# Top-k attention before two expert layers: one TensorE job for a block's transposes, a later block's scores and a query, and exponentials written to SBUF

## The chip, the core and the metric

The kernel runs on one core of a Trainium2 chip. A core has TensorE for matrix products (PE in the profile; its weight loads are a row of their own, PEld), VectorE (DVE), ScalarE (ACT), GpSimd (POOL) and a queue that issues transfers (SP). Each engine works through its own list of instructions in a fixed order; semaphores hold an instruction back until what it needs is there. TensorE writes into PSUM, which has eight banks of 128 x 512 fp32 values; everything else lives in SBUF. The metric is the device time of one execution in microseconds.

## What is computed

Attention with a top-32 mask, then two mixture-of-experts layers, all in fp32:

```python
scores = scale * np.matmul(q, k.transpose(0, 1, 3, 2))      # 2 batches, 8 heads, 576 x 576, head size 64
kth = np.partition(scores, -32, axis=-1)[..., -32:-31]
scores = np.where(scores >= kth, scores, -1e9)
attn = np.exp(scores - np.max(scores, axis=-1, keepdims=True))
attn = attn / (np.sum(attn, axis=-1, keepdims=True) + 1e-9)
x = np.matmul(attn, v)                                       # -> 1152 rows of 512
...
for e in range(8):                                           # first mixture: every row through every expert
    out += P[:, e:e + 1] * (np.maximum(x @ w1[e], 0.0) @ w2[e])
...
# second mixture: each row goes to its best expert, in eight groups
```

P comes from gate logits by an exponential and eight alternating normalisations of rows and columns.

## The kernel before

**Blocks.** Attention is cut into 72 blocks, numbered n from 0. A block is 128 query rows against all 576 keys of one head; where a sequence has only 64 rows left, one block holds 64 rows of two heads. `block` makes the scores of a block, `search` (for n of 16 and more; `search_first` before) finds the 32nd largest score of each row and turns the scores into weights, `values` multiplies the weights with v once all blocks of a pair of heads are through. Blocks 16 to 71 are those that the change touches.

**One block, step by step.** (1) A query tile is transposed on TensorE (128 columns, L257), and ACT and DVE split it into two parts of fp32r, a high and a low one (L598, L606). (2) Scores: two halves of 288 keys, each in a PSUM bank of its own, with two products each, one for each part of the query (four where the block holds two heads; L618); ACT copies each half into the SBUF tile `sc` (L623). (3) The search on DVE: four times the 8 largest (MAX8; L715, L721), and between them three times these 8 taken out (MATCH_REPLACE8, L719). (4) ACT writes the exponentials of each half into a PSUM bank (L728), and DVE multiplies each half with the mask, `e = (sc >= 32nd) * exponential`, with the sum over the row as a by-product (a SCALAR_TENSOR_TENSOR and the read of its accumulator, L730). (5) DVE adds the two sums and takes the reciprocal (L736, L738), ACT scales `e` (L739). (6) TensorE turns `e`: four transposes into one bank, a fifth of 64 rows into another (L257). (7) ACT copies the high parts out of both banks (`eth`, L769), and DVE (L773), or in some blocks GpSimd (L777), writes the low parts (`etl`, and `eth` for the fifth).

**PSUM.** There are four banks named `tp` for attention and four named `yp` for the experts. Early on one `tp` bank is given to the experts (the job of type X at the end of the loop in `visits_first`), so that blocks 16 to 71 share three.

**What stands beside attention.** While attention runs, `visit` feeds the first mixture's experts to TensorE: layer 1 in chunks of four products (L980), layer 2 (L1090), in fp32r, with three products for each pair of high and low parts. Its weights are split by ACT (L918) and GpSimd (L924), its hidden layer by ACT (L932) and DVE (L934). What is not done beside attention is done after it; the amount is the same.

**What sets the order.** Nothing runs in the order of the code: `job` hands a piece of work with an engine, a rank, an estimated cost, the jobs it depends on and the buffers it takes to a planner (`Order`). The planner goes forward in its own estimated time: of the jobs of an engine that can start first, the one of lowest rank is taken and written out, and a job holds its buffers until all that use it have ended in the plan. Attention's jobs rank by block number, the experts' at 1000 and above. Where TensorE would be idle for more than a set time in the plan, `busy` writes idle products in (`ones_b`, L294) that keep it at work and whose result nobody reads. The plan becomes each engine's fixed order; on the chip an engine waits at its next instruction until that can run.

Of the kernel before, what the change touches and what calls it, by code (L numbers as in the profile page):

```python
# [7 lines left out]
F32 = mybir.dt.float32  # L8
# [10 lines left out]
EPS = 1e-9  # L19
# [4 lines left out]
PARTIAL = 2  # L24
FILL = 390.0
# [187 lines left out]
class Net:  # L213
# [208 lines left out]
    def attention(self):  # L422
# [5 lines left out]
        self.attended = []  # L428
        for g, (b, tiles) in enumerate(GROUPS):
            made = []  # L430
            for pair in range(4):
# [20 lines left out]
            self.spans.append((c0, c1, made))  # L452
            for t in range(c0 // 128, -(-c1 // 128)):
                self.xdone.setdefault(t, []).extend(made)
        self.gate_logits()

# [122 lines left out]
    def block(self, x):  # L579
# [16 lines left out]
        def src():  # L596
            return p.t[:, :128].rearrange("p (a c) -> p a c", a=2) if two else p.t[:, :128]
        jh = self.job("ACT", n - 2.9, t_act(128), lambda: nc.scalar.activation(parts(0), src(), AF.Copy),  # L598
                      deps=[j], use=[p, qs])
        if 2 <= n < ALONE:  # L600
            jm = self.job("PE", n - 2.9, 0.12, lambda: nc.tensor.matmul(
                p.t[:, :128], self.minus, parts(0), start=False, stop=True, skip_group_check=True), deps=[jh], use=[p, qs])
            jl = self.job("ACT", n - 2.9, t_act(128), lambda: nc.scalar.activation(parts(1), p.t[:, :128], AF.Copy),
                          deps=[jm], use=[p, qs])
        else:
            jl = self.job("DVE", n - 2.4, t_dve(128), lambda: nc.vector.tensor_sub(  # L606
                parts(1), src(), parts(0).bitcast(F32)), deps=[jh], use=[p])
# [3 lines left out]
        got = []  # L611
        for half in range(2):
            ps = self.psa.box()

            def scores(half=half, ps=ps):
                for m, (s, k) in enumerate(terms):
                    w = qs.t[:, s, k, :] if two else qs.t[:, s]
# [1133 lines left out]
```

## Time and profile before

| | |
|---|---|
| three runs | 1181.81, 1182.82 (median), 1186.1 us |
| the profiled execution | 1184.28 us, of which 1182.5 us from the first to the last instruction |
| busy over the span: PE, PEld, DVE, ACT, POOL | 98%, 85%, 77%, 62%, 35% |
| mean granted clock of TensorE | 0.996 of full speed |
| the first mask of block 16 begins (L730) | 97.7 us |
| the first and the last transpose of `e` in blocks 16 to 71 | 104.37 us, 542.14 us |

A busy share is an average over stages that have different limits. Here the stretch from 104 us to 542 us, in which blocks 16 to 71 run, is to be read apart from what follows, in which DVE and ACT have far less to do. A matrix product counts as busy until its modelled end, which lies behind the start of the next one; how fast TensorE works is read from the distance between starts.

### The profile page before, as it was taken

Reading aid. Unit: us, or ns where it says so; the run is one execution under the profiler, and the core shown is the slowest. Engines: PE = TensorE matmul, PEld = TensorE weight load, DVE = VectorE, ACT = ScalarE, POOL = GpSimd, SP = SyncE. Lnnn points to the kernel's source line nnn. Section 1 sums busy time; section 2 is a strip of 40 time slices with the busy share of each in tenths; the row PEclk is TensorE's granted clock in tenths of the full one; section 3 lists DMA queues with packets and bytes.
Section 4 is the critical chain, followed back from the end, with each engine's and each line's share of the span. In section 5 each row is a group of like instructions: output and inputs, shape, how many; then the busy total and the mean of one; then the engine's idle time right before and its main releaser. Section 6 shows DMA issues by size and latency. Waiting matters only on the chain.

```text
span 1182.5 us, 20945 instructions
## 1 busy us (share of the span) xinstructions
PE 1159.9 (98%) x6619; PEld 1004.2 (85%) x6619; DVE 911.7 (77%) x2194; ACT 734.2 (62%) x1729; POOL 417.9 (35%) x387
## 2 busy tenths in 40 slices
PE   8998999999999999999999999999999999999997
PEld 5866889888888888878888889999999999798886
DVE  7999999999999999995745667754455556468883
ACT  7666889989888977876343335543333445158882
POOL 5464788877656745446000001000000000015541
PEclk9999999999999999999999999999999999999999
DMA  5457775755444664444545546653344444179970
GB/s 142 113 154 199 203 193 171 203 167 157 141 130 119 183 196 131 152 126 131 169 149 185 172 144 194 194 147 115 116 127 131 143 143 147 49 229 362 353 262 23
DMA packets 243032, 194.04 MB, mean 164 GB/s; under 512 B 67487, under 2 KB 186271, under 8 KB 242912
## 3 DMA queue, kind: packets, MB, share of 16 engines
q1 hardware_dynamic: 240656, 187.74, 53.1%
q0 software_dynamic: 1648, 4.73, 1.0%
q8 instruction: 54, 0.88, 0.3%
q14 instruction: 66, 0.54, 0.1%
q10 hardware_dynamic: 608, 0.15, 0.1%
HBM read 172.34 MB, written 20.80 MB: 163 GB/s over the span
## 4 chain that ended last, share of the span: by engine, by line
PE 67%; DVE 17%; issue 5%; ACT 4%; DMA 3%; POOL 2%; SPq 1%; POOLq 0%; another core or an unknown queue 0%; DVEq 0%; ACTq 0%
PE yp L980 23%; PE yp L1090 21%; PE tp L1090 6%; PE tp L980 4%; DVE wk L719 3%; PE tp L257 3%; DVE m L721 3%; PE tp L618 2%; PE tp L809 2%; DVE e L730 1%; DVE wk L665 1%; DVE m L667 1%; DVE hl L934 1%; PE yp L1335 1%; DVE m L715 1%
## 5 line engine op out<-in xcount | busy, mean ns | idle before, releaser
L1702 POOL DMA_INDIRECT disp<-acc,idx x9 | 10.6, 1173 | 465.0 <-DVE run L1698 465.0
L924 POOL TENSOR_TENSOR w0l<-ra,w0h 128x512 fp32r<-128x512 f32 x96 | 124.5, 1297 | 70.7 <-ACT w0h L918 67.5
L924 POOL TENSOR_TENSOR w1l<-rb,w1h 128x512 fp32r<-128x512 f32 x96 | 124.4, 1295 | 61.8 <-ACT w1h L918 54.9
L980 PE MATMUL yp<-xl,w0h 128*128 128x256 f32 (+2 forms) x680 | 142.3, 331 | 0.0
L980 PE MATMUL yp<-xh,w0h 128*128 128x256 f32 (+2 forms) x680 | 141.7, 330 | 0.2 <-ACT w0h L918 0.2
L980 PE MATMUL yp<-xh,w0l 128*128 128x256 f32 (+2 forms) x680 | 141.6, 330 | 0.0
L918 ACT ACTIVATE w0h<-ra 128x512 fp32r<-128x512 f32 x211 | 131.7, 625 | 0.0
L918 ACT ACTIVATE w1h<-rb 128x512 fp32r<-128x512 f32 x148 | 93.0, 629 | 55.4 <-PE yp L1090 47.5
L721 DVE MAX8 m<-wk 128x8 f32<-128x576 f32 x168 | 125.2, 752 | 1.0
L980 PEld LDWEIGHTS yp<-xh,w0h 128*128 128x128 f32 x680 | 113.9, 189 | 11.8 <-ACT w0h L918 0.5
L932 ACT ACTIVATE hh<-yp 128x256 fp32r<-128x256 f32 (+3 forms) x142 | 64.0, 451 | 96.0 <-PE yp L980 78.7
L980 PEld LDWEIGHTS yp<-xh,w0l 128*128 128x128 f32 x680 | 110.7, 189 | 6.5 <-POOL w0l L924 0.4
L980 PEld LDWEIGHTS yp<-xl,w0h 128*128 128x128 f32 x680 | 110.9, 190 | 6.0
L1090 PE MATMUL yp<-w1h,hh 128*128 128x512 f32 x280 | 114.4, 409 | 0.0
L934 DVE SCALAR_TENSOR_TENSOR hl<-yp,hh 128x256 fp32r<-128x256 f32 (+3 forms) x142 | 71.4, 503 | 54.7 <-ACT hh L932 53.9
L1090 PE MATMUL yp<-v,f 128*128 128x512 f32 x480 | 112.4, 392 | 0.0
L1090 PE MATMUL yp<-w1l,hh 128*128 128x512 f32 x280 | 110.2, 393 | 0.0
L1090 PE MATMUL yp<-w1h,hl 128*128 128x512 f32 x280 | 109.8, 392 | 0.0
L1090 PEld LDWEIGHTS yp<-v,f 128*128 128x128 f32 x480 | 89.9, 189 | 18.0
L918 ACT ACTIVATE v<-rb 128x512 fp32r<-128x512 f32 x65 | 40.7, 629 | 77.9 <-PE yp L1090 52.3
L719 DVE MATCH_REPLACE8 wk<-m,wk 128x576 f32<-128x576 f32 x112 | 83.3, 744 | 0.5
L921 DVE TENSOR_TENSOR w0l<-ra,w0h 128x512 fp32r<-128x512 f32 x115 | 79.1, 688 | 1.0
(486 smaller groups left out, 2720.5 us busy)
## 6 DMA issues: line engine op xcount, KB each, us to landing
rb<-in_moe_w_dram SPq DMA_DIRECT2D x248, 256.0 KB
ra<-in_moe_w_dram SPq DMA_DIRECT2D x245, 256.0 KB
acc<-in_moe_w_dram SPq DMA_DIRECT2D x67, 256.0 KB
y<-ys SPq DMA_DIRECT2D x31, 256.0 KB
ys<-y SPq DMA_DIRECT2D x21, 256.0 KB
vr<-in_v_dram SPq DMA_DIRECT2D x40, 128.0 KB
disp<-z SPq DMA_DIRECT2D x6, 771.0 KB
qg<-in_q_dram SPq DMA_DIRECT2D x63, 64.0 KB
```

Source lines behind the costliest of these rows:

```text
L257: self.nc.tensor.transpose(out, in_, self.ident[:p, :p])
L618: nc.tensor.matmul(ps.t[:, :288], w, keys[k][0].t[:, half * 288:(half + 1) * 288], start=m == 0, stop=m == len(terms) - 1)
L719: j = self.job("DVE", r, 0.73, lambda i=i: nc.vector.match_replace(wk.t, m.t[:, i], flat() if i == 0 else wk.t, LOW), deps=[j], take=[wk] ...
L721: j = self.job("DVE", r, 0.66, lambda i=i: nc.vector.max(m.t[:, i + 1], wk.t), deps=[j], use=[wk] if i == 2 else [])
L809: nc.tensor.matmul(p.t[:, :nq], vs.t[:, t].rearrange("p a d -> p (a d)"), hd["et"].t[s][:, t, :nq], start=t == 0 and s == 0, stop=t == 4)
L918: jh = self.job("ACT", -500 + rank, t_act(512, True), lambda r=r, w=w: nc.scalar.activation(w.t[0], r.t, AF.Copy), deps=[j], take=[w])
L921: jl = self.job("DVE", -100 + rank, t_dve(512, True), lambda r=r, w=w: nc.vector.tensor_sub(w.t[1], r.t, w.t[0].bitcast(F32)), deps=[jh], ...
L924: jl = self.job("POOL", -100 + rank if k > 8 * NATIVE + 4 else FIRST - 3, t_pool(512), lambda r=r, w=w: nc.gpsimd.tensor_sub(w.t[1], r.t, ...
L932: jh = self.job("ACT", -1000 + k * 0.001, t_act(b - a), lambda: nc.scalar.activation(h.t[0][:, a:b], p.t[:, :b - a], AF.Relu), deps=deps, ...
L934: jl = self.job("DVE", -1000 + k * 0.001, t_dve(b - a), lambda: nc.vector.scalar_tensor_tensor(h.t[1][:, a:b], p.t[:, :b - a], 0.0, h.t[0] ...
L980: nc.tensor.matmul(p.t[:, :b - a], w1[0].t[i][:, d, :], self.xt[s][:, d, c0 + a:c0 + b], start=m == 0 and d == 0, stop=m == 2 and d == 3)
L1090: nc.tensor.matmul(y[t].t, h.t[i][:, c:c + 128], w2[0].t[s], start=f == 0 and m == 0, stop=f == last and m == 2)
```

## The change

From block 16 on, `search` no longer cuts the exponentials in halves: one ACT instruction writes all 576 into `e` in SBUF, and one DVE instruction masks `e` in place, with both its inputs, `sc` and `e`, in SBUF. The sum needs no addition of halves. The two PSUM banks that held the exponentials are not taken any more.

The new method `together(m)` makes one TensorE job of three things: the scores of block m+3 (both halves), the transpose of the query of block m+4, and the five transposes of `e` of block m, in this order. The query's transpose goes into columns 288 to 415 of the bank with the second half of the scores, the fifth transpose of `e` into the same columns of the bank with the first half. So a joint job takes all three `tp` banks at once, where seven single uses of a bank stood before. It can begin only when all its inputs and banks are there in the plan; what follows it (copies of scores, splits of query and of `e`) depends on the job as a whole. The jobs of `values` are now handed in behind the joint job of the last block of their heads.

```diff
--- before.py
+++ after.py
@@ -22,6 +22,8 @@
 GROUPS = ((0, (0,)), (0, (1,)), (0, (2, 3, 4)), (1, (0, 1)), (1, (2, 3, 4)))
 NATIVE = 2
 PARTIAL = 2
+AHEAD = 3
+GROUPED = AHEAD + 1
...
-                    made += self.values(b, pair, tiles, heads, n - 1)
+                    late.append((n - 1, lambda b=b, pair=pair, tiles=tiles, heads=heads, n=n, made=made:
+                                 made.extend(self.values(b, pair, tiles, heads, n - 1))))
...
+        for m in range(n - GROUPED, n):
+            self.together(m)
...
+    def together(self, m, query=None):
+        turn, rows = self.turns.get(m), self.rows_.pop(m + AHEAD, None)
+        if turn:
+            deps, take, use, cost, tail, _, jobs = turn
+            calls = []
+            tail.append(rows[2][0] if rows else self.psa.box())
+            take = take + ([] if rows else tail)
+            use = use + tail
+            if rows:
+                x, sc, ps, sdeps, stake, suse, scores, _ = rows
+                deps, take, use, cost = deps + sdeps, take + stake, use + suse, cost + 0.14 * 4 * len(x["heads"])
+                calls.append(scores)
+            go = jobs[0]
+            if query:
+                qdeps, qtake, quse, *_ = query
+                deps, take, use, cost = deps + qdeps, take + qtake, use + quse, cost + 0.13
+            def all_(calls=calls, go=go, query=query):
+                for f in calls:
+                    f()
+                if query:
+                    query[3]()
+                go()
+            j = self.job("PE", m, cost, all_, deps=deps, take=take, use=use)
+            if query:
+                query[4](j)
+            jobs[1](j)
+            if rows:
+                rows[7](j)
+        while self.late and self.late[0][0] <= m:
+            self.late.pop(0)[1]()
...
         qs = (self.qz if two else self.qs).box()
-        p = self.psa.box()
+        mine = n >= ROWS + GROUPED
+        p, at = (None, 288) if mine else (self.psa.box(), 0)
+        bank = [p]
         i = 0 if two else x["heads"][0]["i"]
-        j = self.job("PE", n - 3.5, 0.13, lambda: self.tr(p.t[:, :128], qg.t[:, i].rearrange("p s d -> p (s d)")),
-                     deps=[jq], take=[p, qs], use=[qg])
+        mid = []
+        def turn_q():
+            self.tr(bank[0].t[:, at:at + 128], qg.t[:, i].rearrange("p s d -> p (s d)"))
...
+        query = None
+        if not mine:
+            split_q(self.job("PE", n - 3.5, 0.13, turn_q, deps=[jq], take=[p, qs], use=[qg]))
+        else:
+            bank[0] = self.rows_[n - 1][2][1]
+            query = [jq], [qs], [qg, qs], turn_q, split_q
+        if mine:
+            self.together(n - GROUPED, query)
+        self.rows_[n] = (x, sc, banks, mid + [d for _, dd in keys for d in dd], [*banks, sc],
+                         [qs, sc] + [kb for kb, _ in keys], lambda: [scores(0), scores(1)], finish)
+        return
...
-        masks = []
-        for half in range(2):
-            p = self.psa.box()
-            je = self.job("ACT", r - 0.4, t_act(288, True, 1), lambda half=half, p=p: nc.scalar.activation(
-                p.t[:, :288], sc.t[:, half], AF.Exp, bias=st.t[:, 0:1], scale=0.125), deps=[jb, near], take=[p] if half else [p, e], use=[e])
-            masks.append(self.job("DVE", r, t_dve(288) + 0.08, lambda half=half, p=p: nc.vector.scalar_tensor_tensor(
-                e.t[:, half * 288:(half + 1) * 288], sc.t[:, half], m.t[:, 3, 7:8], p.t[:, :288], op0=OP.is_ge,
-                op1=OP.mult, accum_out=st.t[:, 1 + half:2 + half]), deps=[j, je],
-                use=[p, sc, e, m]))
+        je = self.job("ACT", r - 0.4, t_act(576, True, 1), lambda: nc.scalar.activation(
+            e.t, flat(), AF.Exp, bias=st.t[:, 0:1], scale=0.125), deps=[jb, near], take=[e], use=[e])
+        masks = [self.job("DVE", r, t_dve(576, True), lambda: nc.vector.scalar_tensor_tensor(
+            e.t, flat(), m.t[:, 3, 7:8], e.t, op0=OP.is_ge, op1=OP.mult, accum_out=st.t[:, 1:2]), deps=[j, je],
+            use=[sc, e, m])]
         def total():
-            nc.vector.tensor_scalar(st.t[:, 3:4], st.t[:, 1:2], st.t[:, 2:3], EPS, op0=OP.add, op1=OP.add)
+            nc.vector.tensor_scalar(st.t[:, 3:4], st.t[:, 1:2], EPS, None, op0=OP.add)
...
-        for t0, t1, rows in ((0, 4, 128), (4, 5, 64)):
-            p, nt = self.psa.box(), t1 - t0
-
-            def turn(p=p, t0=t0, t1=t1, rows=rows):
-                for t in range(t0, t1):
-                    self.tr(p.t[:rows, (t - t0) * 128:(t - t0 + 1) * 128], e.t[:, t * 128:t * 128 + rows])
...
+        p = self.psa.box()
+        fresh = [hd["et"] for hd in heads if "et_done" not in hd]
+        for hd in heads:
+            hd.setdefault("et_done", [])
+        tail = []
+        def turn():
+            for t in range(5):
+                rows, o, b = (128, t * 128, p) if t < 4 else (64, 288, tail[0])
+                self.tr(b.t[:rows, o:o + 128], e.t[:, t * 128:t * 128 + rows])
+        def split(j):
+            for t0, t1, rows in ((0, 4, 128), (4, 5, 64)):
+                nt = t1 - t0
+                b, o = (p, 0) if t0 == 0 else (tail[0], 288)
...
+        self.turns[n] = [[jn], [p] + fresh, [e], 0.11 * 5, tail, (None, None), (turn, split)]```

Counted over the whole program (one of the three ways in which the second mixture can go runs in an execution), the change removes 56 DVE and 56 ACT instructions; TensorE's real work is the same, with 47 idle products in place of 40.

The first place is TensorE's list around one block (tile `e_171`): the numbers behind the names are buffers, `qg` is a query tile, `kst` are keys, `qs` a split query, `w0`, `w1` and `h` belong to the experts. Before:

```order
L618 MATMUL tp_65<-kst_156,qs_163 128x288 x2
L257 MATMUL tp_66<-ident,e_171 128x128 x4
L1090 MATMUL yp_69<-w1h_87,hh_95 128x512
...
L257 MATMUL tp_65<-ident,e_171 64x128
L980 MATMUL yp_71<-xh,w0h_79 128x256 x4
...
L1090 MATMUL tp_67<-w1l_90,hh_97 128x512
L1090 MATMUL tp_67<-w1h_89,hl_98 128x512
L618 MATMUL tp_68<-kst_156,qs_163 128x288 x2
L257 MATMUL tp_65<-ident,qg_142 128x128
```

And now, at the same block:

```order
L1162 MATMUL yp_69<-w1h_89,hl_98 128x512
L1162 MATMUL yp_69<-w1h_87,hh_97 128x512
...
L1052 MATMUL yp_72<-xl,w0h_81 128x256 x4
L1052 MATMUL yp_72<-xh,w0l_82 128x256 x4
L667 MATMUL tp_65<-kst_156,qs_163 128x288 x2
L667 MATMUL tp_68<-kst_156,qs_163 128x288 x2
L259 MATMUL tp_68<-ident,qg_141 128x128
L259 MATMUL tp_66<-ident,e_171 128x128 x4
L259 MATMUL tp_65<-ident,e_171 64x128
L1162 MATMUL yp_69<-w1h_89,hh_93 128x512
```

The halves of the scores, the query and the two groups of transposes stood in five places with the experts' products between them, and now stand in one.

The second place is DVE's list around the masks of one block (`e_171`; `st` are the sums, `wk` and `m` the search, `hl` the experts' hidden layer). Before:

```order
L730 SCALAR_TENSOR_TENSOR e_171,st_181<-sc_168,m_177,tp_66 128x288
L719 MATCH_REPLACE wk_169<-m_174,sc_165 128x576
L730 SCALAR_TENSOR_TENSOR e_171,st_181<-sc_168,m_177,tp_65 128x288
L934 SCALAR_TENSOR_TENSOR hl_94<-yp_70,hh_93 128x256
L736 TENSOR_SCALAR st_181<-st_181 128x1
L721 MAX m_174<-wk_169 128x8
L738 RECIPROCAL st_181<-st_181 128x1
```

And now:

```order
L797 SCALAR_TENSOR_TENSOR e_171,st_181<-sc_168,m_177,e_171 128x576
L789 MATCH_REPLACE wk_169<-m_174,sc_165 128x576
L802 TENSOR_SCALAR st_181<-st_181 128x1
L844 TENSOR_TENSOR etl_185<-tp_66,eth_184 128x4x128
L844 TENSOR_TENSOR eth_184<-tp_65,eth_184 64x128
L804 RECIPROCAL st_181<-st_181 128x1
L1006 SCALAR_TENSOR_TENSOR hl_98<-tp_67,hh_97 128x256
```

One mask stands where two stood; the third operand was a bank, `tp`, and is `e` in SBUF.

The third place is where TensorE's list leaves the last block's transposes. Before:

```order
L1090 MATMUL tp_67<-w1h_91,hl_94 128x512
L257 MATMUL tp_65<-ident,e_171 128x128 x4
L257 MATMUL tp_68<-ident,e_171 64x128
L257 MATMUL tp_66<-ident,lgt 128x128
L980 MATMUL yp_70<-xh,w0h_83 128x256 x4
```

And now:

```order
L1052 MATMUL yp_71<-xl,w0h_83 128x256 x4
L1052 MATMUL yp_71<-xh,w0l_84 128x256 x4
L259 MATMUL tp_65<-ident,e_171 128x128 x4
L259 MATMUL tp_68<-ident,e_171 64x128
L1162 MATMUL yp_72<-w1h_91,hh_95 128x512
L1162 MATMUL yp_72<-w1l_92,hh_95 128x512
```

Counted from the start of the list to this point there were 684 layer-1 products of 256 columns and 672 layer-2 products; now there are 732 and 690 ahead of it, while those of other shapes, the scores (312), the products with v (198) and the transposes of `e` (360) are as many as before.

## Rows read from the trace of the kernel before

**Rows 1.** Busy time of each engine by stretch of the span.

```profile
core 0: us, PE busy (x) PEld busy (x) DVE busy (x) ACT busy (x) POOL busy (x), PEclk, DMA share, GB/s
...
104.37:542.14 437.77, 430.89 (x2571) 372.61 (x2572) 427.21 (x1148) 363.51 (x925) 288.19 (x271) 1.00 0.56 161
542.14:1182.50 640.36, 631.59 (x3448) 560.65 (x3446) 389.42 (x825) 300.01 (x592) 75.32 (x60) 1.00 0.53 169
```

**Rows 2.** DVE's waits, 97.7 to 542.14 us: total, times, longest; six lines.

```profile
DVE hl L934 <- ACT hh L932: 1.9, 1, 1.9
...
DVE prob L900 <- PE tp L257: 0.4, 1, 0.4
```

**Rows 3.** What weight loads waited for, 104.37 to 542.14 us.

```profile
PEld tp L257 <- DVE eth L773: 2.9, 5, 1.4
PEld tp L257 <- ACT e L739: 2.4, 4, 0.9
PEld tp L618 <- DVE etl L773: 1.9, 7, 0.4
...
PEld tp L618 <- DVE e L730: 1.4, 5, 0.5
```

**Rows 4.** Groups of TensorE instructions, 104.37 to 542.14 us.

```profile
L1090 PE MATMUL yp<-w1h,hh 128*128 128x512 f32 x168 | 70.0, 417 | 0.0
...
L980 PE MATMUL yp<-xl,w0h 128*128 128x256 f32 x196 | 32.7, 290 | 0.0
```

**Rows 5.** TensorE in order of time: start, length, instruction.

```profile
120.33 0.39 PE L1090 MATMUL tp<-w1h,hl 128*128 128x512 f32 x1
120.55 0.64 PE L980 MATMUL yp<-xh,w0h 128*128 128x256 f32 x4
121.03 0.64 PE L980 MATMUL yp<-xl,w0h 128*128 128x256 f32 x4
...
311.05 0.42 PE L618 MATMUL tp<-kst,qs 128*128 128x288 f32 x2
311.31 0.40 PE L1090 MATMUL yp<-w1h,hh 128*128 128x512 f32 x1
```

**Rows 6.** DVE in order of time around one block's masks.

```profile
315.23 0.50 DVE L730 SCALAR_TENSOR_TENSOR e<-sc,m,tp 128x288 f32<-128x288 f32 x1
...
315.65 0.51 DVE L730 SCALAR_TENSOR_TENSOR e<-sc,m,tp 128x288 f32<-128x288 f32 x1
...
316.09 0.29 DVE L606 TENSOR_TENSOR qs<-tp,qs 128x128 fp32r<-128x128 f32 x1
316.29 0.21 DVE L736 TENSOR_SCALAR st<-st 128x1 f32<-128x1 f32 x1
316.41 0.08 DVE L719 MATCH_VALUE_LOAD wk<-m,sc 128x8 f32 x1
```

**Rows 7.** DVE around a mask of 576 in SBUF (block 7).

```profile
51.27 0.80 DVE L685 SCALAR_TENSOR_TENSOR e<-sc,m,e 128x576 f32<-128x576 f32 x1
51.98 0.75 DVE L667 MAX8 m<-wk 128x8 f32<-128x576 f32 x1
```

**Rows 8.** DVE in the second mixture, both inputs in SBUF.

```profile
1060.99 1.36 DVE L1406 TENSOR_TENSOR xh<-acc,xh 128x512 fp32r<-128x512 f32 x1 [0.28 <-ACT xh L1400]
...
1064.00 0.67 DVE L1406 TENSOR_TENSOR xh<-acc,xh 128x512 fp32r<-128x512 f32 x1
...
1064.93 1.61 DVE L1406 TENSOR_TENSOR xh<-acc,xh 128x512 fp32r<-128x512 f32 x1
```

**Rows 9.** GpSimd in the same stretch.

```profile
1060.51 1.28 POOL L1403 TENSOR_TENSOR f<-acc,f 128x512 fp32r<-128x512 f32 x1 [2.31 <-ACT f L1400]
1064.70 1.30 POOL L1403 TENSOR_TENSOR xh<-acc,xh 128x512 fp32r<-128x512 f32 x1 [2.90 <-DVE xh L1406]
```

**Rows 10.** Groups of GpSimd instructions, 97.7 to 542.14 us.

```profile
L924 POOL TENSOR_TENSOR w0l<-ra,w0h 128x512 fp32r<-128x512 f32 x92 | 119.4, 1297 | 67.6 <-ACT w0h L918 64.4 <-DMA vr<-in_v_dram 1.0 <-POOL eth L777 0.8
L924 POOL TENSOR_TENSOR w1l<-rb,w1h 128x512 fp32r<-128x512 f32 x91 | 117.9, 1296 | 57.3 <-ACT w1h L918 50.3 <-PE tp L257 3.6 <-POOL eth L777 0.9
```

More of the change, by code (lines that the diff above doesn't have):

```diff
@@ L452, in attention @@
             self.spans.append((c0, c1, made))
+        for m in range(n - GROUPED, n):
+            self.together(m)
+        for c0, c1, made in self.spans:
             for t in range(c0 // 128, -(-c1 // 128)):
@@ L610, in block @@
         sc = self.sc.box()
-        got = []
-        for half in range(2):
[L613 to L617, printed above, removed]
-                    nc.tensor.matmul(ps.t[:, :288], w, keys[k][0].t[:, half * 288:(half + 1) * 288],
-                                     start=m == 0, stop=m == len(terms) - 1)
-            j = self.job("PE", n - 2 + 0.1 * half, 0.14 * len(terms), scores,
-                         deps=[jh, jl] + [d for _, dd in keys for d in dd], take=[ps] if half else [ps, sc],
-                         use=[qs, sc] + [kb for kb, _ in keys])
-            got.append(self.job("ACT", n - 1.9 + 0.1 * half, t_act(288), lambda half=half, ps=ps: nc.scalar.activation(
-                sc.t[:, half], ps.t[:, :288], AF.Copy), deps=[j], use=[ps, sc]))
@@ L625, in block, with scores, copied @@
-        (self.search_first if n < ROWS else self.search)(x, sc, got)
+        banks = [self.psa.box() for _ in range(2)]
+        def scores(half):
+            ps = banks[half]
+            for m, (s, k) in enumerate(terms):
+                w = qs.t[:, s, k, :] if two else qs.t[:, s]
+                nc.tensor.matmul(ps.t[:, :288], w, keys[k][0].t[:, half * 288:(half + 1) * 288],
+                                 start=m == 0, stop=m == len(terms) - 1)
+        def copied(half, j):
+            return self.job("ACT", n - 1.9 + 0.1 * half, t_act(288), lambda: nc.scalar.activation(
+                sc.t[:, half], banks[half].t[:, :288], AF.Copy), deps=[j], use=[banks[half], sc])
@@ new lines, in finish @@
+        def finish(j):
+            (self.search_first if n < ROWS else self.search)(x, sc, [copied(half, j) for half in range(2)])
+        if n < ROWS + AHEAD:
+            split_q(self.job("PE", n - 3.5, 0.13, turn_q, deps=[jq], take=[p, qs], use=[qg]))
+            got = []
+            for half in range(2):
+                j = self.job("PE", n - 2 + 0.1 * half, 0.14 * len(terms), lambda half=half: scores(half),
+                             deps=mid + [d for _, dd in keys for d in dd], take=[banks[1]] if half else [banks[0], sc],
+                             use=[qs, sc] + [kb for kb, _ in keys])
+                got.append(copied(half, j))
+            return (self.search_first if n < ROWS else self.search)(x, sc, got)
@@ new lines, in block @@
+        query = None
+        if not mine:
+            split_q(self.job("PE", n - 3.5, 0.13, turn_q, deps=[jq], take=[p, qs], use=[qg]))
+        else:
+            bank[0] = self.rows_[n - 1][2][1]
[4 more added lines that the diff above has]
+                         [qs, sc] + [kb for kb, _ in keys], lambda: [scores(0), scores(1)], finish)
@@ L781, in values @@
+        self.turns[n] = [[jn], [p] + fresh, [e], 0.11 * 5, tail, (None, None), (turn, split)]
     def values(self, b, pair, tiles, heads, n):
```

82 lines of the change are left out of this document (41 added, 41 removed).

## Prediction

> **What bounds the kernel now.** I read the stretches first [rows 1]. Between 104 and 542 us, while blocks 16 to 71 run, DVE is busy for 427.2 of 437.8 us, and TensorE's products look as full with 430.9. After 542 us TensorE is busy for 631.6 of 640.4 us and DVE for 389.4, so the rest of the kernel is TensorE's alone. Which of the two leads in the attention stage is seen from their waits. DVE hardly waits for anyone: six lines, from 1.9 us down to 0.4 us, 5.7 us together [rows 2]. TensorE's weight loads do wait, and mostly for DVE: for a bank that the split of the turned weights gives back (2.9 us for the transposes, 1.9 us for the scores), for a bank that a mask gives back (1.4 us), for the scaled `e` (2.4 us) [rows 3]. A second reading says the same. Where nothing is in the way, a layer-2 product takes 0.23 us up to the next start, four layer-1 products of 256 columns take 0.48 us, so one 0.12 us, and two scores 0.26 us, so one 0.13 us [rows 5]. The groups of [rows 4] are parts of 672 layer-2 products and 684 of those layer-1 products in this stretch; with each form counted at its own distance, TensorE's list from the first to the last transpose of `e` is worth 416 us. The 22 us between that and 437.8 are waits and restarts after them, hidden under the modelled ends. So in the attention stage DVE leads, TensorE follows with some slack, and a saving on DVE or a burden on it decides; outside the stage only TensorE's amount of work counts.
>
> One more fact of the order matters. The expert work is constant, so what is done beside attention is missing afterwards. The new list holds 48 more layer-1 products and 18 more layer-2 products before the last transposes of `e`: 48 x 0.12 + 18 x 0.23 = 9.9 us. The time of the whole therefore changes by what the stage's end changes, less 9.9 us.
>
> **The change part by part.**
>
> *Two masks become one.* Now two masks of 288 begin at 315.23 and 315.65 us and the next instruction begins at 316.09 us: 0.86 us a block [rows 6]. The trace has the new form twice in the first blocks, a mask of 576 with both inputs in SBUF: from 51.27 to the next start at 51.98 us, 0.71 us [rows 7]. That saves 0.15 us, in 56 blocks 8.4 us of DVE. Both have GpSimd idle beside them.
>
> *The sum of the halves goes.* The instruction stays, with one operand less. It takes 0.12 us up to the next start now [rows 6]; the saving lies between nothing and 6.7 us in all, and I take nothing, since what remains is an instruction on one column too.
>
> *The mask's second input moves from PSUM to SBUF.* This is the part that can cost. In the second mixture DVE subtracts 512 columns with both inputs in SBUF. One such takes 0.67 us at 1064.00 us. Two that begin while GpSimd is inside an instruction of its own take 1.36 and 1.61 us [rows 8]; GpSimd's two began at 1060.51 and 1064.70 us and ended at 1061.79 and 1066.00 us [rows 9]. Each time DVE ends 0.55 us after GpSimd does. So DVE stood still until GpSimd was through: 0.69 us more where 0.80 us of GpSimd's instruction was left, 0.94 us where 1.07 us was left, in short the remainder less 0.12 us. Before the change no mask of blocks 16 to 71 could meet this, since one input was a bank. In the stage GpSimd splits expert weights, 92 and 91 times 1.30 us [rows 10], which is 237 of 444 us. A mask that begins at any moment meets one with a chance of 0.53 and then waits 0.65 - 0.12 = 0.53 us: 0.28 us. GpSimd's other instructions, some 51 of the 288.2 us that it is busy [rows 1], are mostly shorter and add about 0.04 us. An estimate of 0.32 us a mask, 18 us for 56. The bounds are nothing, if the mask with its accumulator doesn't stand still as the subtractions do, and 30 us, if each mask meets a weight split. I take 18.
>
> The Trainium skill speaks of this in "SBUF — State Buffer", section "Who interferes with whom": a VectorE instruction with two inputs in SBUF takes its second one through a read interface that GpSimd shares, whoever starts first keeps it to its end, and an instruction with at most one SBUF input is not concerned. By that rule every mask pays and the old ones never did, which by the same row counts is the 18 us above; without it the mask would be the plain saving of 8.4 us. The traced subtractions agree with the rule; no row shows a mask beside GpSimd.
>
> *One exponential of 576 for two of 288.* ACT is busy for 363.5 us of the stage [rows 1] and no one's leader; what it saves is worth nothing here, being under DVE's work. If ACT led, it would be worth about what the joined mask saves on DVE, 8 us.
>
> *Five TensorE jobs become one.* The instructions are the same and none is cheaper: a product after a transpose costs its own length. What can go is waiting: seven uses of a bank become three, and the waits for masks' banks vanish. On the other side the job takes all three banks at once and stands behind the latest of its inputs, the scaled `e` of its block; the scores in it are wanted by DVE only three blocks later, so that DVE doesn't starve. As DVE leads, TensorE's lost waits buy nothing by themselves, except that DVE's own 5.7 us of waits for ACT's copies shrink. I take 2 us of them (bounds 0 and 5.7).
>
> *Seven more idle products*, 7 x 0.23 = 1.6 us, stand where the plan saw TensorE idle; in a stage that DVE leads they are covered by that idleness and cost nothing. Uncovered they cost 1.6 us.
>
> **The sum.** DVE's stage: - 8.4 + 18 - 2 = + 7.6 us. Less the 9.9 us of expert work that has moved into it: - 2.3 us. The profiled execution took 1184.28 us, 1.78 us more than its span and 1.46 us above the median of 1182.82. So 1182.0 us for that execution, 1180.5 us beside the median: I say 1181 us. A difference under 0.5%, 5.9 us, I count as no change; that is about what can be told apart here.
>
> **The rivals.**
>
> *TensorE leads (faster).* If masks don't stand still, or seldom, DVE has 427 - 8.4 = 419 us to do and TensorE 416 + 9.9 = 426 us. Then the joint jobs count: with one place to wait at in each block instead of five, and no bank given back by a mask, perhaps half of the 22 us of waits is left. Stage 426 + 11 = 437 us, 1 us less than now; with the 9.9 us and 1.6 us for idle products that is - 9 us, 1174 us beside the median. If a third of the waits is left, 1170 us; if none, 1162 us. For it speaks that waits for banks are the larger part of [rows 3]; against it, rows 8 and 9, where each subtraction that met GpSimd stood still.
>
> *The joint job passes DVE's halts on (slower).* The planner counts the mask at its undisturbed length and has already spent DVE's saving on the 9.9 us of expert work. A mask held up by 0.32 us delays the scaled `e`, the joint job behind which all of TensorE stands, layer 1 behind that, and DVE itself where it comes to the next split of a hidden layer; then nothing of the halts is made up in DVE's planned gaps, neither the 8.4 us nor the 2 us. The stage grows by the full 18 us: + 18 - 9.9 + 1.6 = + 9.7 us, 1193 us beside the median. It decides from the point on at which the halts are more than the 9.9 us plus the 5.9 us of the bound, some 0.28 us a mask, with nothing made up. Against it: the scores are three blocks ahead, and DVE's list has other blocks' searches between a mask and what waits for it.
>
> *The grouping does nothing*, since TensorE starts the same instructions and DVE sets the pace: this is inside my forecast, where its worth is 2 us.
>
> **How the numbers follow.** My forecast, halts on DVE and most of them paid for by the saving and the moved expert work, has 0.43 and covers 1175 to 1188 us, with halts from 12 to 24 us. TensorE leading has 0.33, 1165 to 1176 us; halts passed on, 0.24, 1188 to 1196 us. A range that leaves out no more than the outer parts of both, 2 in 10, is 1169 to 1193 us. Faster by over 0.5% means below 1176.9 us: 0.34, the first rival and the low end of the forecast. Slower, above 1188.7 us: 0.23. Between them 0.43.
>
> **What the profile after would show.** The mask's mean length should be about 0.8 + 0.3 us, spread from 0.8 to 2.1 us, the long ones ending a fixed time after a GpSimd instruction does; if all are 0.8 us, the first rival stands. DVE should be busy, halts included, for nearly all of the stage, and the last transpose of `e` should end near 550 us. Waits of weight loads for masks should be gone, and waits for the scaled `e` should have grown in their place. I should be wrong if TensorE's list turned out to wait for something that I hold to be early, such as keys, a query's transfer or the experts' weights from a GpSimd that DVE holds up in turn.

## The result, and the profile after

The changed kernel takes 1192.93 us (median of 6 runs, 1190.96 to 1193.24), the kernel before 1184.6 us on the same chip. The ratio is 1.0074, with a 95% interval of 1.0061 to 1.0088: slower by 0.74%, 8.8 us. I had said 1181 us and no change; the time lies at the very edge of my range, 1169 to 1193 us. The profiled execution of the changed kernel spans 1191.0 us, 8.5 us more than before. The first fence answers to [rows 1]: the stage, cut at the same 104.37 us, and what follows it.

```profile
104.37:561.67 457.30, 439.41 (x2642) 386.69 (x2639) 439.13 (x1042) 353.99 (x882) 309.68 (x277) 1.00 0.55 159
561.67:1191.00 629.33, 621.49 (x3381) 551.41 (x3379) 387.14 (x821) 293.30 (x580) 67.89 (x54) 1.00 0.53 168
```

The last transpose of `e` ends at 561.67 us instead of 542.14 us: 19.5 us later, where I had + 7.6. The rest of the kernel is 11.0 us shorter (640.36 to 629.33), as 9.9 us of moved expert work asked for. So what went wrong lies in the stage alone. DVE's column (the third behind the length) splits it: busy for 439.13 us (+ 11.9 on [rows 1]), idle for 18.2 us (+ 7.6).

DVE's waits between 104.37 and 561.67 us (total, times, longest) answer to [rows 2]; I had hoped to lose 2 us there:

```profile
DVE etl L844 <- ACT eth L840: 5.5, 4, 1.8
DVE m L785 <- ACT sc L671: 2.9, 6, 0.5
```

The first line is a low part that waits for ACT's copy of the turned weights, the second a search that waits for its scores: what the joint job delivers comes later than DVE could take it. The waits of the weight loads in the same stretch answer to [rows 3]:

```profile
PEld tp L667 <- DVE kst L569: 4.3, 5, 1.4
...
PEld tp L259 <- ACT e L805: 3.0, 5, 1.1
PEld tp L667 <- DVE eth L844: 2.8, 4, 1.2
PEld tp L667 <- DVE xr L886: 2.7, 4, 1.1
```

No wait for a mask's bank is left, as forecast. The wait for the scaled `e` has hardly grown (2.4 to 3.0 us). New are waits of the scores (L667), which now head the joint job, for DVE's splits of keys (`kst`) and for `xr`, a sum of `values`. Neither is an input that these scores were short of. The lists show what they wait for: ahead of such a wait DVE's last two key splits write `kst_151` and read banks `tp_68` and `tp_66`, and the joint job behind them writes its scores into `tp_68` and `tp_66`, from other keys (`kst_152`). All five waits for `kst` are of this kind, and the sum `xr` reads a bank too. The joint job waits for the last of its three banks. One place in order of time, from three engines:

```profile
145.76 0.23 DVE L569 TENSOR_TENSOR kst<-tp,kst 64x64 fp32r<-64x64 f32 x1
...
146.04 0.53 PE L667 MATMUL tp<-kst,qs 128*128 128x288 f32 x2 [1.15 <-DVE kst L569]
...
147.61 0.58 ACT L840 ACTIVATE eth<-tp 128x512 fp32r<-128x512 f32 x1
...
148.21 0.69 DVE L844 TENSOR_TENSOR etl<-tp,eth 128x512 fp32r<-128x512 f32 x1 [1.85 <-ACT eth L840]
```

The key split stands behind a mask that was halted (1.38 us from 144.33 us on), the joint job waits for its bank, and DVE then stands idle for 1.85 us until ACT has copied what the job turned.

The masks were halted as forecast. DVE and GpSimd in order of time (start, length) show one, as [rows 8, 9] did for other instructions:

```profile
206.95 1.69 DVE L797 SCALAR_TENSOR_TENSOR e<-sc,m,e 128x576 f32<-128x576 f32 x1
...
206.73 1.30 POOL L996 TENSOR_TENSOR w1l<-rb,w1h 128x512 fp32r<-128x512 f32 x1
207.98 1.82 POOL L996 TENSOR_TENSOR w0l<-ra,w0h 128x512 fp32r<-128x512 f32 x1
```

The mask begins 0.22 us after GpSimd's instruction and ends at 208.64 us, 0.61 us after that one's end at 208.03 us. GpSimd's next takes 1.82 us instead of 1.30: it stands still in its turn. The group of all 56 masks (sum, mean in ns):

```profile
L797 DVE SCALAR_TENSOR_TENSOR e<-sc,m,e 128x576 f32<-128x576 f32 x56 | 61.3, 1095 | 0.8
```

Undisturbed they take 46.1 us (run e9 below), so the halts are 15.2 us, 0.27 us each, where I had 18 us and 0.32. Of the 56 masks 25 take more than 1 us, and every one of these ends 0.61 or 0.62 us after an instruction of GpSimd does.

### The profile page after: what moved, and what is told of

The parts are those of the page before. It is cut to its first block, busy times and chain, and to the rows that moved or that the text cites. A ratio compares the mean times of both kernels' runs of the same rounds, so it can differ in the third digit from the quotient of the medians.

```text
span 1191.0 us, 20741 instructions
## 1 busy us (share of the span) xinstructions
PE 1157.4 (97%) x6626; PEld 1008.7 (85%) x6626; DVE 921.2 (77%) x2082; ACT 717.7 (60%) x1673; POOL 432.3 (36%) x387
## 4 chain that ended last, share of the span: by engine, by line
PE 55%; DVE 28%; ACT 5%; issue 5%; POOL 3%; DMA 3%; SPq 1%; POOLq 0%; DVEq 0%; ACTq 0%
PE yp L1162 18%; PE yp L1052 17%; DVE wk L789 6%; DVE m L791 5%; PE tp L1052 5%; PE tp L1162 4%; DVE e L797 3%; DVE hl L1006 2%; PE tp L259 2%; DVE m L785 2%; DVE wk L735 2%; DVE m L737 1%; DVE etl L844 1%; DMA ra<-in_moe_w_dram 1%; PE yp L1381 1%
## 5 line engine op out<-in xcount | busy, mean ns | idle before, releaser
L996 POOL TENSOR_TENSOR w0l<-ra,w0h 128x512 fp32r<-128x512 f32 x96 | 129.4, 1348 | 84.7 <-ACT w0h L990 79.1
L996 POOL TENSOR_TENSOR w1l<-rb,w1h 128x512 fp32r<-128x512 f32 x96 | 128.2, 1335 | 42.7 <-ACT w1h L990 33.2
L1052 PE MATMUL yp<-xh,w0h 128*128 128x256 f32 (+2 forms) x648 | 132.4, 326 | 1.3 <-DVE hl L1006 0.9
L1052 PE MATMUL yp<-xh,w0l 128*128 128x256 f32 (+2 forms) x648 | 131.7, 325 | 0.7 <-POOL w0l L996 0.7
L1052 PE MATMUL yp<-xl,w0h 128*128 128x256 f32 (+2 forms) x648 | 132.1, 325 | 0.0
L1052 PEld LDWEIGHTS yp<-xh,w0h 128*128 128x128 f32 x648 | 108.3, 188 | 13.5 <-DVE hl L1006 1.7
L1162 PE MATMUL yp<-w1h,hh 128*128 128x512 f32 x288 | 115.6, 401 | 1.2 <-ACT hh L1004 1.2
L1162 PE MATMUL yp<-w1l,hh 128*128 128x512 f32 x288 | 113.0, 392 | 0.4 <-POOL w1l L996 0.4
L1162 PE MATMUL yp<-w1h,hl 128*128 128x512 f32 x288 | 112.7, 391 | 0.0
L1162 PE MATMUL yp<-v,f 128*128 128x512 f32 x480 | 112.6, 392 | 0.0
L1052 PEld LDWEIGHTS yp<-xh,w0l 128*128 128x128 f32 x648 | 105.1, 189 | 5.9 <-POOL w0l L996 0.9
L1052 PEld LDWEIGHTS yp<-xl,w0h 128*128 128x128 f32 x648 | 104.9, 189 | 4.9
L1162 PEld LDWEIGHTS yp<-v,f 128*128 128x128 f32 x480 | 90.0, 189 | 18.0
L1004 ACT ACTIVATE hh<-yp 128x256 fp32r<-128x256 f32 (+2 forms) x134 | 59.2, 442 | 73.8 <-PE yp L1052 55.7
L1006 DVE SCALAR_TENSOR_TENSOR hl<-yp,hh 128x256 fp32r<-128x256 f32 (+2 forms) x134 | 66.1, 493 | 41.3 <-ACT hh L1004 40.8
L789 DVE MATCH_REPLACE8 wk<-m,wk 128x576 f32<-128x576 f32 x112 | 83.3, 744 | 0.2
```

What stands on the lines that cost most here:

```text
L789: j = self.job("DVE", r, 0.73, lambda i=i: nc.vector.match_replace(wk.t, m.t[:, i], flat() if i == 0 else wk.t, LOW), deps=[j], take=[wk] ...
L996: jl = self.job("POOL", -100 + rank if k > 8 * NATIVE + 4 else FIRST - 3, t_pool(512), lambda r=r, w=w: nc.gpsimd.tensor_sub(w.t[1], r.t, ...
L1004: jh = self.job("ACT", -1000 + k * 0.001, t_act(b - a), lambda: nc.scalar.activation(h.t[0][:, a:b], p.t[:, :b - a], AF.Relu), deps=deps, ...
L1006: jl = self.job("DVE", -1000 + k * 0.001, t_dve(b - a), lambda: nc.vector.scalar_tensor_tensor(h.t[1][:, a:b], p.t[:, :b - a], 0.0, h.t[0] ...
L1052: nc.tensor.matmul(p.t[:, :b - a], w1[0].t[i][:, d, :], self.xt[s][:, d, c0 + a:c0 + b], start=m == 0 and d == 0, stop=m == 2 and d == 3)
L1162: nc.tensor.matmul(y[t].t, h.t[i][:, c:c + 128], w2[0].t[s], start=f == 0 and m == 0, stop=f == last and m == 2)
```

## The experiments

Each time stands beside the kernel before on the same chip; since the chips differ a little, runs are compared with each other by their ratios. Unless a run's expectation says otherwise, the whole computation is done.

| run | median, us | ratio to before, 95% interval |
|---|---|---|
| changed kernel | 1192.93 | 1.0074 (1.0061 to 1.0088) |
| e1_sbuf_only | 1208.49 | 1.0213 (1.0200 to 1.0226) |
| e2_joint_only | 1196.69 | 1.0114 (1.0099 to 1.0129) |
| e3_before_memset | 1182.43 | 0.9992 (0.9983 to 1.0001) |
| e4_after_memset | 1179.55 | 0.9967 (0.9955 to 0.9980) |
| e5_sbuf_memset | 1184.70 | 1.0019 (1.0010 to 1.0028) |
| e6_before_dve | 1193.89 | 1.0086 (1.0073 to 1.0099) |
| e7_before_pe | 1184.31 | 1.0006 (0.9997 to 1.0015) |
| e8_after_memset_dve | 1186.83 | 1.0031 (1.0019 to 1.0044) |
| e9_after_long | 1178.34 | 0.9948 (0.9936 to 0.9961) |
| e10_after_uneven | 1191.33 | 1.0057 (1.0042 to 1.0072) |
| e11_after_two | 1191.83 | 1.0068 (1.0051 to 1.0085) |
| e12_after_four | 1224.28 | 1.0351 (1.0334 to 1.0369) |
| e13_long_pe | 1182.66 | 0.9998 (0.9988 to 1.0009) |
| e14_after_pe | 1193.58 | 1.0100 (1.0080 to 1.0119) |
| e15_after_cost | 1198.98 | 1.0138 (1.0120 to 1.0156) |

**Are the halts the loss, or the joint job?** Theory H says that the masks' halts cost what was lost; the rival J, that the joint job costs by itself. First each half of the change alone. e1 puts the new mask into the kernel before:

```diff
-        for half in range(2):          # two exponentials into banks, two masks of 288
+        je = ... nc.scalar.activation(e.t, flat(), AF.Exp, ...)
+        masks = [... nc.vector.scalar_tensor_tensor(e.t, flat(), m.t[:, 3, 7:8], e.t, ...)]
```

> Only the first half of the change: one exponential of 576 columns into SBUF and one mask with both inputs in SBUF; scores, query transposes and the transposes of e stay five separate TensorE jobs. Theory H (GpSimd halts the masks, some 16 us over 56 masks, and nothing makes up for them): masks of 1.1 us on average as in the changed kernel, and a time about 7 to 16 us above the kernel before. Theory J (the joint job is what costs: its scores wait for keys, banks and e, whatever the masks do): masks of 1.1 us too, but the separate jobs take them up, and the time is within 3 us of the kernel before.

e2 puts the old lines of that diff into the changed kernel.

> Only the second half of the change: the joint TensorE job, with exponentials still in two PSUM banks and two masks of 288 with one input in SBUF, so that no mask can meet GpSimd. Theory H: no halts, so nothing to pass on: the time is 0 to 8 us below the kernel before. Theory J: the joint job's own waits stay, and the masks' banks come back into the game: 5 to 10 us above the kernel before.

Both halves lost more alone than together: + 25.6 and + 13.8 us. Neither theory had that. So the halts had to be taken away with all else in place, by a GpSimd instruction that writes the same tile and reads nothing from SBUF:

```diff
-                jl = self.job("POOL", ..., lambda: nc.gpsimd.tensor_sub(w.t[1], r.t, w.t[0].bitcast(F32)), ...)
+                jl = self.job("POOL", ..., lambda: nc.gpsimd.memset(w.t[1].bitcast(F32), 0.0), ...)
```

> The kernel before, in which GpSimd fills the low parts of the experts' weights with zeros instead of subtracting them (so the low parts are left out of the result); the instruction reads nothing from SBUF and is shorter, some 0.6 us instead of 1.30. It is the ground for the next run. No mask here has two SBUF inputs, so both theories expect the time of the kernel before, to 2 us, a little less if experts' weights were ever late from GpSimd.

> The changed kernel with the same filling instead of subtracting, so that a mask with two SBUF inputs meets hardly a GpSimd instruction that reads SBUF. Theory H: masks of about 0.82 us, and the time falls to 2 to 9 us below that of the kernel before with the same filling, where the changed kernel stands about 8.5 us above the kernel before. Theory J: masks of about 0.82 us as well, but the time stays 5 to 9 us above the kernel before with the same filling.

> The first half of the change alone (single exponential and single mask in SBUF, separate TensorE jobs), with GpSimd filling the low parts of the weights with zeros (they are left out of the result), so that masks are not halted. Alone and halted it took 25.6 us more than the kernel before, with 67.8 us in masks against 46 to 47 us undisturbed. Theory H (halts are passed on whole, by whichever jobs): about 21 us less than that, 1186 to 1190 us. Theory P (the separate jobs, planned with less expert work in the stage, cost by themselves, and halts are only a part): 1196 to 1206 us.

e3 stays at the time of before, and e4 falls 12.7 us (1.07%) below the changed kernel, to 0.33% below before. In e9 GpSimd fills two and a half times, so that it is at work as long as with the subtraction:

```diff
-                    w.t[1], r.t, w.t[0].bitcast(F32))
+                    flat2(w.t[1])[:, :c].bitcast(F32), 0.0) for c in (512, 512, 256)]      # nc.gpsimd.memset
```

> The changed kernel with GpSimd filling zeros again (the low parts of the weights are left out of the result), but two and a half times each, an estimate of 1.35 us as for the subtraction: GpSimd is as long at work as in the changed kernel and reads nothing from SBUF. Theory H (what costs is that masks stand still): masks of about 0.83 us and the time of the run with short filling, 1178 to 1182 us. Theory G (weights late from a slow GpSimd are a part of the loss): 1184 to 1190 us.

The stage's window and the group of the masks in e9:

```profile
104.37:548.50 444.13, 436.17 (x2652) 387.63 (x2650) 425.24 (x1046) 356.11 (x886) 306.76 (x653) 1.00 0.56 165
```

```profile
L801 DVE SCALAR_TENSOR_TENSOR e<-sc,m,e 128x576 f32<-128x576 f32 x56 | 46.1, 823 | 0.8
```

GpSimd is busy for 306.8 us (last engine column) and masks take 0.82 us all the same: it is its reading that halts them. The time is 14.9 us (1.26%) below that of the changed kernel, for 15.2 us of halts. Weights late from a slow GpSimd (theory G) are next to no part of it; a filling does not wait for ACT's high part as a subtraction does, but in the changed kernel weight loads wait for GpSimd's low parts for only 1.7 us in the whole stage. Here the halts are passed on whole, and not only by the joint job: with separate jobs the masks of e1 and e5 are

```profile
L727 DVE SCALAR_TENSOR_TENSOR e<-sc,m,e 128x576 f32<-128x576 f32 x56 | 67.0, 1196 | 0.6
```

```profile
L727 DVE SCALAR_TENSOR_TENSOR e<-sc,m,e 128x576 f32<-128x576 f32 x56 | 47.4, 847 | 0.6
```

19.6 us more in the masks and 23.0 us (1.94%) more in the time; GpSimd is also at work for less long in e5, which may have a part in it. So theory H holds for the halts. J holds for another part: without halts the change is worth 6 us (0.52%), where my sum without its halts is 20 us. The stage windows of e5 (new mask, separate jobs, no halts) and of e2 (joint job, old masks) show where DVE's waits come from:

```profile
104.37:529.10 424.73, 416.94 (x2508) 359.17 (x2508) 417.95 (x1037) 347.35 (x864) 147.54 (x264) 1.00 0.55 161
```

```profile
104.37:572.70 468.33, 457.98 (x2747) 399.78 (x2748) 443.49 (x1165) 373.20 (x954) 299.98 (x280) 1.00 0.56 163
```

DVE is idle for 6.8 us with separate jobs, for 24.8 us with joint jobs and old masks, for 18.9 us with both (e9), for 10.6 us before [rows 1]. The joint job brings waits, with exponentials in banks or without. (The plans of e2 and e5 also move expert work, 21 us into the stage and 15 us out of it, so only the idle time is compared.) Expert work is not what DVE waits for in e9: of its named waits 9.5 us are for ACT's copies of turned weights and scores, which the joint job delivers, and 2.0 us for a hidden layer. In e5 the copies account for 1.6 us, before for 2.1 us.

**Who leads the stage?** A dummy search on DVE (a maximum over 128 columns) behind each block's masks, and an idle product of 512 columns (0.23 us up to the next start) ahead of each block's transposes; neither is known to the planner.

```diff
+                nc.vector.max(self.extra, flat()[:, :128])                     # e6, e8; e10: 412 columns, every second block
+                nc.tensor.matmul(p.t, b, b[:, None, :].to_broadcast([128, 4, 128]), start=True, stop=True)   # e7, e13, e14
```

> The kernel before with a dummy search for a maximum over 128 columns behind the second mask of each of the 56 blocks, unknown to the planner: an estimate of 0.25 us each, 14 us of DVE. It puts the delay of the halts into the kernel before. Theory D (DVE leads in the stage, as I predicted, so its time counts whole): 12 to 15 us more. Theory T (TensorE leads, DVE has room): 0 to 6 us more. Theory B (the two are coupled block by block, and either one's delay is passed on): 12 to 15 us more here, and as much in the run with idle products.

> The kernel before with one idle product of 512 columns ahead of the four transposes of each of the 56 blocks, unknown to the planner: 0.23 us each, 12.9 us of TensorE. Theory D (DVE leads, TensorE has some 22 us of waits to hide it in): 0 to 4 us more. Theory T (TensorE leads): 10 to 13 us more. Theory B (coupled): 10 to 13 us more.

The dummy search is 0.29 us long, but the next instruction starts before it ends. Two lines of e8 show it:

```profile
302.35 0.29 DVE L802 MAX8 extra<-sc 128x8 f32<-128x128 f32 x1
302.56 0.54 DVE L1010 SCALAR_TENSOR_TENSOR hl<-yp,hh 128x384 fp32r<-128x384 f32 x1
```

It takes 0.21 us of DVE, so the burden is not 56 x 0.29 = 16.2 us, as the expectation of e10 has it, but 11.7 us. In the kernel before, these 11.7 us of DVE cost 0.86%, 10 us, and 12.7 us of TensorE cost 1 us: DVE leads there and its burden counts nearly whole, as the prediction read from [rows 2, 3].

> The changed kernel without halts (long filling of GpSimd, low parts left out), with one idle product of 512 columns ahead of the five transposes of each of the 56 blocks, 12.7 us of TensorE unknown to the planner, which cost the kernel before 0 to 2 us. Theory T (without halts TensorE leads, so the mask's saving is worth little): 9 to 13 us above the 1178.3 us of the same kernel without them. Theory D (DVE still leads): 0 to 4 us above it.

> The changed kernel as it is, halts and all, with the same 12.7 us of idle products. Theory C (the halts are passed on whole because TensorE is already full and the job has no slack): 8 to 13 us above the changed kernel. Theory D (with halts DVE leads the stage again, and TensorE stands idle while masks are halted): 0 to 4 us above it.

Without halts the same 12.7 us cost 0.50%, 5.9 us, more than theory D allows and less than theory T: TensorE absorbs only half of it, but it doesn't lead alone. With halts they cost 0.26%, some 3 us by the ratios, with overlapping intervals: TensorE has room again while masks stand still.

> The changed kernel without halts (GpSimd fills zeros, the weights' low parts are left out of the result) and with the same dummy search of 0.25 us on DVE behind each mask: it gives the masks' delay back without GpSimd. Theories D and B (delay of DVE is passed on whole): 12 to 15 us above the 1179.6 us of the kernel without halts, so the time of the changed kernel again. Theory T (without halts TensorE leads and DVE has room): 0 to 7 us above it. Theory G (it is GpSimd, held up by the masks in turn, that is late with weights): 0 to 4 us above it.

> The changed kernel without halts (short filling, low parts left out) and a dummy search on DVE again, 16.2 us in all, but as 0.58 us in every second block instead of 0.29 us in each. The even one cost 7.3 us. Theory U (uneven delays are passed on more fully than even ones, which is why 15 us of halts cost 13 us): 10 to 14 us above the kernel without halts. Theory E (only the sum of the delay counts): 6 to 9 us above it.

Against e4 the even burden costs 0.64%, 7.6 us of 11.7: less than theories D and B said, a little more than T. The uneven one costs 0.90%, 10.7 us. But the two burdens are not equal, as theories U and E take them to be: a search over 412 columns takes 0.51 us up to the next start, in 28 blocks 14.3 us. By share that is 65% and 75%, no difference beyond the intervals. So without halts neither engine leads alone, each absorbs a quarter to a half of what is put on it. That uneven delays are passed on more fully is not shown, and why the halts cost all of their 15.2 us stays open.

**Can the halts be shortened or planned for?** GpSimd's subtraction in two or four pieces, and the mask planned 0.3 us longer:

```diff
+                    flat2(w.t[1])[:, c:c + 128], flat2(r.t)[:, c:c + 128], ...) for c in range(0, 512, 128)]   # e12; e11: 256
-        masks = [self.job("DVE", r, t_dve(576, True), ...
+        masks = [self.job("DVE", r, t_dve(576, True) + 0.3, ...                                                 # e15
```

> The changed kernel with each low part of the weights subtracted by GpSimd in two instructions of 256 columns, an estimate of 0.74 us each by the values' rows; the whole computation, same plan. If a halt lasts to the end of the GpSimd instruction that is under way, halts shrink to about half: 7 to 9 us in the masks instead of 16, and by theory H the time falls by 6 to 8 us to 1184 to 1188 us. If GpSimd keeps the port between its instructions, or its longer work (0.2 us more for each weight) makes weights late, it stays at 1190 to 1196 us.

> The same with four instructions of 128 columns, an estimate of 0.46 us each: halts of some 4 to 6 us in the masks and by theory H 1181 to 1186 us. GpSimd then has about 100 us more to do in the stage, over 400 of 456 us; if weights come late from it (theory G), 1190 to 1205 us.

> The changed kernel with the mask planned 0.3 us longer (0.98 instead of 0.68 us) and nothing else; the plan then puts more expert work beside attention (30 layer-2 and 36 layer-1 products more before the last transposes of e, 11.1 us, and 29 more idle products, 6.6 us). Theory N (the planner's ignorance is a part of the loss): 1182 to 1188 us. Theory H (halts come unevenly and no plan catches them): 1190 to 1200 us.

None of the three helped. In e11 the masks' halts shrink to 10.1 us, 5.1 us less, but the stage is only 1.8 us shorter and the time stays within its interval. One mask there stands for 4.98 us, from 176.77 to 181.75 us. Behind it TensorE ran dry, and its clock fell:

```profile
181.70:183.90 2.20, 0.12 (x1) 0.12 (x2) 2.14 (x9) 0.07 (x1) 0.00 (x0) 1.00 0.74 228
183.90:187.30 3.40, 3.13 (x9) 2.14 (x10) 3.26 (x7) 3.21 (x6) 2.07 (x3) 0.50 0.01 2
```

TensorE is busy for 0.12 of 2.20 us and is then granted half its clock (0.50, 1.2 of 2.4 GHz) for 3.4 us; in the changed kernel it keeps the full clock throughout the stage. That is a part of what the shorter halts did not bring; the rest is open. In e12 the halts grow. DVE and then GpSimd there, in order of time (GpSimd's row gathers four instructions, the last of a row of such):

```profile
220.33 9.12 DVE L801 SCALAR_TENSOR_TENSOR e<-sc,m,e 128x576 f32<-128x576 f32 x1
...
227.14 1.69 POOL L1000 TENSOR_TENSOR w0l<-ra,w0h 128x128 fp32r<-128x128 f32 x4
```

One mask takes 9.12 us. It stands still through 19 further GpSimd instructions that follow each other without a gap, and ends 0.62 us after the last of them (227.14 + 1.69 = 228.83). So a halt doesn't always end with the instruction under way. Five masks of e12 stand for over 4.6 us, and about the end of each of them TensorE, which had run dry, is granted half its clock for 3.4 or 6.8 us; this comes on top of the halts in the 33 us that e12 loses against the changed kernel. In e15 the plan took in 11 us more expert work, met GpSimd more often (66.4 us in the masks) and lost 7.6 us (0.64%) more, as theory H had it: the planner's ignorance was not the loss.

## Why the prediction was wrong

**What bounds the kernel before: right.** DVE leads and TensorE follows with slack (e6, e7). The slack is of another kind than I read, though. I wrote that a product after a transpose costs its own length, and that the 22 us beyond TensorE's list are waits. The trace of the kernel before says otherwise:

```profile
111.06 0.72 PE L257 MATMUL tp<-ident,e 128*128 128x128 f32 x5
111.54 0.48 PE L1090 MATMUL tp<-w1h,hh 128*128 128x512 f32 x1
111.86 0.40 PE L1090 MATMUL tp<-w1l,hh 128*128 128x512 f32 x1
112.09 0.39 PE L1090 MATMUL tp<-w1h,hl 128*128 128x512 f32 x1
```

The product behind the transposes takes 0.32 us up to the next start, the one behind it 0.23 us. Between 120 and 500 us the median is 0.314 us for the 50 high-part layer-2 products that follow a transpose and 0.231 us for the others. The stage has 137 such places before the change and 63 after it, so by these numbers an estimate of 11 of the 22 us were this price, and the joint job saves TensorE some 6 us for which my sum has no term. In a stage that DVE leads (e7) they buy little.

**The mask in SBUF is halted by GpSimd: right, 15.2 us for 18.** Mean 1.095 us for a forecast of 1.1, from 0.80 to 1.87 us. The Trainium skill's rule in "SBUF — State Buffer", section "Who interferes with whom", agrees twice over: masks are halted by GpSimd's subtractions, and not by its fillings, which only write (e9). That whoever started first gives way at the end of its instruction holds in the changed kernel; e12 shows that the one waiting may then still not get its turn.

**The moved expert work: right.** 9.9 us forecast, and the rest of the kernel is 11.0 us shorter.

**The step that failed is the "- 2" in the sum, the price of making five TensorE jobs into one, and with it the "- 8.4", which was there but was not left over.** I reasoned that the scores, made three blocks ahead, would keep DVE fed and that fewer waits for banks could only help. So I booked 10.4 us off the stage beside the halts. Without halts (e9) the stage is 6.4 us longer than before, 444.13 for 437.77: an error of 16.8 us. DVE is idle there for 8.3 us more, not 2 us less, which is 10 us of the error. And it is busy for 2.0 us less, not 8.4. The saving itself came: counted up to the next start, masks and sums take 8.5 us less than before (masks 47.3 to 41.2 us; sums, which I had put at nothing, 7.1 to 4.7 us). But DVE's other instructions take 6 to 7 us more. Of that, 1.4 us are four more splits of a hidden layer, moved in with the expert work and forgotten in my sum, and as much is one more step of a search inside the later cut. The remaining 4 us or so are longer distances to the next start of the same instructions.

Waits and longer distances both go with the joint job, not with the mask. With the new mask and separate jobs (e5), DVE is idle for 3.8 us less than before, and its other instructions take as long as before (0.5 us less in all). With the joint job and the old masks (e2) it is idle for 14.3 us more, and they take 9 us more. The job stands behind the latest of a block's scaled `e` and of its three banks, one of which DVE itself may still hold, and DVE then waits for what it delivers. How much of this belongs to the banks and how much to the rest of the grouping was not separated.

The halts then add 13.9 us to DVE's busy time (425.24 to 439.13) and 13.2 us to the stage. - 2.0 + 8.3 + 13.2 = + 19.5 us, the measured end.

**The rivals.** *The joint job passes DVE's halts on* had the time, 1193 us, and half the reason. Halts are passed on whole, and the savings did not pay for them. But the joint job is not what passes them on (e1 against e5 does so without it), planning for them doesn't help (e15), and the rival has no term for DVE's new waits: that its number fits to the microsecond is luck. The evidence that I set against it, scores three blocks ahead and other blocks' searches in between, absorbed next to none of the halts. *TensorE leads* is near to what happens without halts: I gave it 1174 us, e4 and e9 have 1179.6 and 1178.3, and TensorE then absorbs only half of a burden (e13). My mistake was to hold these two for alternatives, halts with a saving that pays for them or no halts and TensorE in the lead. In fact the loss by halts and the loss by the joint job stood one on top of the other.

**What it should have shown.** Of the signs that I named, the mask's length, its end a fixed time after GpSimd's and the vanished waits for its banks came; the last transpose near 550 us, DVE without idle time and a clearly grown wait for `e` did not. The longest new wait is at the splits of keys, which I named as what would make me wrong, but it is for the banks that they hold and not for keys. That the job takes all three banks at once stands in my prediction, without a price. Whether an earlier split of the keys, or a bank of their own, would give back a part of the 8.3 us was not tried.

## What to carry to other kernels

Before an operand is moved from PSUM to SBUF to save an instruction, look at what GpSimd reads at that time: 0.11 us saved in each mask cost 0.27 us in halts. When jobs are joined, price the latest of their inputs and of their buffers, and what each consumer then waits for, not the number of waits that go. And count a short instruction up to the next start, not by its length: 0.29 us of a dummy search were 0.21 us of DVE. Where two engines were as nearly balanced as here, a saving on one went into new waits while the loss stayed, so the two should not be set off against each other in a sum.

## What the runs showed of the hardware that was not expected

A DVE instruction halted by GpSimd may stand through many GpSimd instructions, if they follow without a gap: 9.12 us for a mask of 0.82 us (e12). Cutting GpSimd's work into four made it worse, 81.8 us in 56 masks for 61.3 us, although other masks there got in after one or two of the short ones. The halt works both ways: GpSimd's next instruction took 1.82 us for 1.30. Behind the longest halts TensorE ran dry and was granted half its clock (e11, e12). And a product right behind a transpose takes 0.08 us more up to the next start than behind another product, at 256 columns (0.201 for 0.120 us) as at 512 (0.314 for 0.231 us).
